# A delta-rule attention with a feed-forward layer: the planned order of the work replaced by an order laid by hand in a table

## The chip, the cores and the metric

The kernel runs on one core of a Trainium2 chip. Its time is the device time of one execution in microseconds (us). TensorE is called PE in the rows (PEld is its weight load), VectorE is DVE, ScalarE is ACT, SyncE is SP; SP issues nearly all DMAs.

## The reference

`q`, `k`, `v` are 4 sequences x 8 heads x 768 positions x 48, `beta` is 4 x 8 x 768. Each of the 32 heads keeps a 48 x 48 state; the output of every position, heads side by side, goes through a feed-forward layer.

```python
k_n = k / (norm(k) + 1e-6)
for t in range(S):
    y[t] = q[t] @ state
    state = state + beta[t] * outer(k_n[t], v[t] - state.T @ k_n[t])
x = y.transpose(0, 2, 1, 3).reshape(3072, 384)
h = x @ w_in                                    # 384 -> 2048
return maximum(0.01 * h, h) @ w_out             # 2048 -> 384
```

## The kernel before, in words

**Blocks.** The 768 positions are cut into 12 blocks of 64 (C). Within a block the recurrence is solved in closed form, which needs the inverse T of a unit-triangular 64 x 64 matrix for each of the 32 heads; from block to block only the state is carried. Block n's 256 rows (4 sequences x 64) then go through the feed-forward layer. The heads are handled in two groups (g = 0, 1) of 16.

**The chain of one block** (functions and lines of the kernel before):
- `gram` (L169): loads kq, forms the products k k^T and k q^T on PE (pg, L198, 32 matmuls a group), copies the first to gs on ACT (L202), writes its triangles to DRAM (gd, L207, four small DMAs a group) and reads them back with one head per partition as L (L222). DVE masks the second product into rq (L214) and keeps a corner in gm (L218).
- `inv` (L270): `norms` (L229 to L249, small DVE operations, from L237 on), then `eliminate` (L251): 31 steps, each of up to four DVE operations (L261 and L266). The first two blocks are inverted together, their 32 heads each filling 128 partitions with two 32 x 32 halves; every later block alone, spread over 128 partitions by halves of the rows.
- `bounce` (L305): T goes to DRAM (td; for later blocks also transposed, tt, after an ACT copy at L298).
- `merge` (L322): reads T back (rt, gm), for the first two blocks transposes it on PE (pt, L337, copied by DVE at L338), and joins the two halves by two products: pz (L354, copied to zs by ACT and DVE, L356) and pu (L364, copied into rt by ACT, L370, and DVE, L368).
- `solve` (L378): pn (L382) and nt; loads k, v, q; `kt` (pk, L407; ACT copies L409; DVE scales v at L413), `step_w` (pw, L421; copies L426), `step_s` (pc, L434; L436), `step_y` (py, L444; ys, L446).
- `columns` (L469): px (L477) turns ys into columns, split into xh (ACT, L118) and xl (DVE, L119).

**The feed-forward layer** (`ffn`, L484): 16 steps f. A step is nine ph matmuls (L504) with 256 columns, then ACT's gh and ph (L508, L509), DVE's gl (L511), and, two steps later, six po matmuls (L494) with 384 columns, whose sums stay in two PSUM banks over the block. At the block's end ACT copies po to ob (L525) and SP sends it out.

**Weights.** 16 tiles of 768 KB (`load_w`) come as 64-bit floats and are taken apart into a high and a low part by seven operations each (`weights`, L127: ACT at L140, L144, L153, DVE at L142, L146, L148, L155).

**What sets the order.** The program is traced by generators that `weave` (L536) interleaves by shares: in each block of feed-forward steps some steps of the weights, of the chain of block n + 1, of the inverse of block n + 2 and of the Grams of block n + 3. The compiler then orders each engine's instructions by a schedule that it simulates (`schedule_with_timeline_sim=True`), held by edges "issue this behind that" (`behind`, table `AFTER`). PSUM: two banks for po, two for ph, four (`ps_a`) that the chain shares.

Of the kernel before, what the change touches and what calls it, by code (L numbers as in the profile page):

```python
# [50 lines left out]
def delta_moe_kernel(ctx: ExitStack, tc, kqT, kv, qT, beta, cst, w_all, out, nblk):  # L51
# [75 lines left out]
    def weights():  # L127

        for f in range(NFC):
            raw = raws.pop(f)
            mid = raw[:, 0:8 * DO].bitcast(U32).rearrange("p (n two) -> p two n", two=2)[:, 1]
            top = raw[:, 4:].rearrange("p (n four) -> p four n", four=4)[:, 0]
            n = sb.tile([P, 2 * DO], BF16, tag="ca", name=f"ca{f}", bufs=2)
            g = sb.tile([P, 2 * DO], F32, tag="cg", name=f"cg{f}", bufs=CB)
            gi, gt = g.bitcast(U32), g.bitcast(U16).rearrange("p (n two) -> p two n", two=2)[:, 1]
            at = iter(AFTER.get(f, AFTER[None]))
            with behind(next(at)):
                nc.scalar.activation(n, top.bitcast(BF16), AF.Abs)  # L140
            with behind(next(at)):
                nc.vector.tensor_scalar(n, n, A_MIN, A_MAX, ALU.max, ALU.min)  # L142
            with behind(next(at)):
                nc.scalar.activation(g.bitcast(I32), n.bitcast(U16), AF.Copy, bias=-float(TOP_MIN << 19), scale=float(1 << 19))  # L144
            with behind(next(at)):
                nc.vector.scalar_tensor_tensor(gi, mid, 13, gi, ALU.logical_shift_right, ALU.bitwise_or)  # L146
            with behind(next(at)):
                nc.vector.scalar_tensor_tensor(gt, top, 0x8000, gt, ALU.bitwise_and, ALU.bitwise_or)  # L148
            t = sb.tile([P, 2, 2 * DO], F32R, tag=f"w{f}", name=f"w{f}", bufs=1)
            for k in range(2):  # L150
                wi[k][f], wo[k][f] = t[:, k, :DO], t[:, k, DO:]
            with behind(next(at)):
                nc.scalar.copy(t[:, 0], g)  # L153
            with behind(next(at)):
                nc.vector.tensor_tensor(t[:, 1], g, t[:, 0].bitcast(F32), ALU.subtract)  # L155
# [490 lines left out]
```

## Time and profile before

| | us |
|---|---|
| median of three runs | 697.28 (696.96 to 698.68) |
| the profiled execution | 697.9 |
| its span, first to last instruction | 696.1 |
| PE busy | 620.6 (89%) |
| DVE busy | 473.6 (68%) |
| ACT busy | 328.7 (47%) |

The profile is of one execution. Busy times are sums over the whole span; the stages differ, so the rows below are taken by stage. A row such as `384.32 0.39 PE L504 ...` gives start and length in us of a run of like instructions; matmuls overlap, so their distance is read from start to start.

### The profile page before, as it was taken

Reading aid. Unit: us, or ns where it says so; the run is one execution under the profiler, and the core shown is the slowest. Engines: PE = TensorE matmul, PEld = TensorE weight load, DVE = VectorE, ACT = ScalarE, POOL = GpSimd, SP = SyncE. Lnnn points to the kernel's source line nnn. Section 1 sums busy time; section 2 is a strip of 40 time slices with the busy share of each in tenths; the row PEclk is TensorE's granted clock in tenths of the full one; section 3 lists DMA queues with packets and bytes.
Section 4 is the critical chain, followed back from the end, with each engine's and each line's share of the span. In section 5 each row is a group of like instructions: output and inputs, shape, how many; then the busy total and the mean of one; then the engine's idle time right before and its main releaser. Section 6 shows DMA issues by size and latency. Waiting matters only on the chain.

```text
span 696.1 us, 20962 instructions
## 1 busy us (share of the span) xinstructions
PE 620.6 (89%) x8424; PEld 579.2 (83%) x8424; DVE 473.6 (68%) x2050; ACT 328.7 (47%) x811; POOL 7.4 (1%) x12
## 2 busy tenths in 40 slices
PE   4102989779999999999999999999999999999996
PEld 3102878679999999999999999999999999999996
DVE  6898599797965957947857758759759759431221
ACT  2221688424555445544634634635535544544432
POOL 4000000000000000000000000000000000000000
PEclk9999989969999999999999999999999999999999
DMA  8797611374055074072172271380370440410001
GB/s 204 179 402 146 221 25 25 69 160 67 7 92 137 4 134 97 14 146 74 36 141 57 48 150 35 61 168 5 73 157 3 82 102 3 70 24 3 12 13 24
DMA packets 126274, 60.39 MB, mean 87 GB/s; under 512 B 112992, under 2 KB 116192, under 8 KB 126176
## 3 DMA queue, kind: packets, MB, share of 16 engines
q1 hardware_dynamic: 123456, 57.86, 36.7%
q10 hardware_dynamic: 2720, 1.18, 0.9%
q8 instruction: 66, 1.08, 0.6%
q14 instruction: 32, 0.26, 0.1%
HBM read 46.70 MB, written 12.32 MB: 85 GB/s over the span
## 4 chain that ended last, share of the span: by engine, by line
PE 78%; DMA 9%; DVE 8%; ACT 2%; issue 1%; SPq 1%; ACTq 0%; DVEq 0%
PE ph L504 30%; PE po L494 27%; DMA wr<-in_w_all 5%; PE pw L421 3%; PE py L444 3%; PE pk L407 3%; PE pu L364 2%; PE pg L198 2%; DVE rv L413 2%; PE pc L434 2%; PE pz L354 2%; PE px L477 2%; DMA kq<-in_kqT 2%; DMA L<-gd 1%; DVE cg L146 1%
## 5 line engine op out<-in xcount | busy, mean ns | idle before, releaser
L504 PE MATMUL ph<-xh,w 128*128 128x256 f32 x1152 | 249.8, 291 | 5.7 <-DVE gl L511 5.6
L504 PEld LDWEIGHTS ph<-xh,w 128*128 128x128 f32 x1152 | 192.5, 191 | 13.9 <-DVE gl L511 8.0
L494 PE MATMUL po<-w,gh 128*128 128x384 f32 x768 | 191.7, 345 | 3.6 <-ACT gh L508 3.6
L511 DVE TENSOR_TENSOR gl<-ph,gh 128x256 fp32r<-128x256 f32 x192 | 81.1, 424 | 134.7 <-ACT ph L509 125.6
L504 PE MATMUL ph<-xl,w 128*128 128x256 f32 x576 | 166.1, 289 | 0.6
L508 ACT ACTIVATE gh<-ph 128x256 fp32r<-128x256 f32 x192 | 73.8, 385 | 150.3 <-PE ph L504 148.6
L494 PEld LDWEIGHTS po<-w,gh 128*128 128x128 f32 x768 | 132.6, 191 | 5.8 <-ACT gh L508 5.6
L494 PE MATMUL po<-w,gl 128*128 128x384 f32 x384 | 119.4, 343 | 0.0
L266 DVE TENSOR_TENSOR T<-T,tmp 128x60 f32<-128x60 f32 (+35 forms) x661 | 112.6, 208 | 1.3
L261 DVE TENSOR_TENSOR tmp<-T,L 128x60 f32<-128x60 f32 (+35 forms) x661 | 112.7, 208 | 0.8
L504 PEld LDWEIGHTS ph<-xl,w 128*128 128x128 f32 x576 | 110.0, 191 | 3.1 <-DVE xl L119 2.2
L509 ACT ACTIVATE ph<-ph 128x256 f32<-128x256 f32 x192 | 72.9, 380 | 0.0
L494 PEld LDWEIGHTS po<-w,gl 128*128 128x128 f32 x384 | 67.9, 189 | 0.5
L214 DVE TENSOR_TENSOR rq<-pg,csb 64x256 f32<-64x256 f32 x96 | 40.6, 423 | 18.8 <-ACT gs L202 17.6
L198 PE MATMUL pg<-kq 48*64 48x128 f32 x768 | 35.8, 306 | 13.8 <-DMA kq<-in_kqT 4.9
L198 PEld LDWEIGHTS pg<-kq 48*64 48x64 f32 x768 | 28.8, 150 | 20.2 <-DMA kq<-in_kqT 5.7
L337 PE MATMUL pt<-csb,rt 32*32 32x32 f32 x128 | 6.8, 215 | 33.3 <-DMA rt<-td 33.3
L337 PEld LDWEIGHTS pt<-csb,rt 32*32 32x32 f32 x128 | 5.9, 129 | 33.7 <-DMA rt<-td 33.4
L409 ACT ACTIVATE rt<-pk 48x512 f32<-48x512 f32 x44 | 26.1, 594 | 14.8 <-PE pk L407 14.1
L202 ACT COPY gs<-pg 128x256 f32<-128x256 f32 x48 | 15.8, 376 | 33.0 <-PE pg L198 27.0
L426 ACT COPY rv<-pw 64x384 f32<-64x384 f32 x46 | 21.8, 474 | 17.3 <-PE pw L421 16.4
L413 DVE TENSOR_TENSOR rv<-rv,nt 64x384 f32<-64x384 f32 x48 | 23.7, 555 | 8.8 <-ACT nt L384 8.7
(61 smaller groups left out, 634.4 us busy)
## 6 DMA issues: line engine op xcount, KB each, us to landing
wr<-in_w_all SPq DMA_DIRECT2D x16, 768.0 KB, 10.2
kq<-in_kqT SPq DMA_DIRECT2D x44, 192.0 KB, 4.2
L<-gd SPq DMA_DIRECT2D x22, 256.0 KB, 3.9
rk<-in_kv SPq DMA_DIRECT2D x24, 192.0 KB, 3.2
rv<-in_kv SPq DMA_DIRECT2D x24, 192.0 KB, 4.2
rq<-in_qT SPq DMA_DIRECT2D x24, 192.0 KB, 4.1
out<-ob SPq DMA_DIRECT2D x48, 96.0 KB, 2.8
rt<-td SPq DMA_DIRECT2D x48, 64.0 KB, 2.7
```

Source lines behind the costliest of these rows:

```text
L198: nc.tensor.matmul(ps[b][c * 64:(c + 1) * 64, p * 128:(p + 1) * 128], kq[r, c ^ b, p, 0], kq[r, c ^ b, p].rearrange("p x t -> p (x t)"), s ...
L214: nc.vector.tensor_tensor(qa[DN, c, b * NPAIR:(b + 1) * NPAIR], pv[b][r, 1], tri[r].rearrange("p (o t) -> p o t", o=1).broadcast_to([C, NP ...
L261: nc.vector.tensor_tensor(tv, t[:, :, j:j + 1].broadcast_to([P, k, w]), L[:, j, j + 1:].rearrange("p (o w) -> p o w", o=1).broadcast_to([P ...
L266: i = nc.vector.tensor_tensor(t, t, tv, ALU.subtract)
L409: nc.scalar.mul(t[UP, c], pv[c * 64:c * 64 + D], -1.0)
L413: nc.vector.tensor_tensor(v[DN, :, us], v[DN, :, us], nt[DN, g, :, us].rearrange("p h (u o) -> p h u o", o=1).broadcast_to([C, 2, NPAIR, D ...
L426: i = nc.scalar.copy(v[DN, c], pv[c * 64:c * 64 + C])
L494: i = nc.tensor.matmul(po[t][:, :DO], a[:, ts_], w[f], start=(f == 0 and k == 0), stop=(f == NFC - 1 and k == 2))
L504: nc.tensor.matmul(ph, a[f][:, cc * P:(cc + 1) * P], x[cc][e], start=(k == 0), stop=(k == 3 * NCC - 1))
L508: nc.scalar.activation(gh, ph, AF.Prelu, alpha=0.01)
L509: i = nc.scalar.activation(ph, ph, AF.Prelu, alpha=0.01)
L511: i = nc.vector.tensor_tensor(gl, ph, gh.bitcast(F32), ALU.subtract)
```

## The change

The generators, `weave`, `AFTER` and `behind` go. The program is traced under `tc.manual_schedule()`, so that each engine runs its instructions in the order of the text, and that order comes from a table with one entry for each feed-forward step: what stands before the bar is played ahead of the step's ph, what follows it after the step's po. Letters are chain parts, for both groups unless a digit follows, `e*3` is three steps of the inverse of block n + 2, `f` of block n + 1, `w` seven conversion steps, `@` names a block.

```diff
+    both = {
+        "A": (1, load_t), "B": (2, load_kv), "C": (1, turn), "Z": (1, merge_z), "U": (1, merge_u),
+        "V": (1, values), "K": (1, step_k), "W": (1, step_w), "S": (1, step_s), "Y": (1, step_y),
+        "P": (1, halves_a), "H": (1, halves_b), "J": (1, halves_c),
+        "G": (3, gram), "O": (3, gram_out), "R": (3, gram_rest), "M": (3, gram_corner)}
+    once = {
+        "Q": (3, loads_kq), "I": (3, gram_in), "D": (2, bounce), "N": (1, turn_norms), "X": (1, columns),
+        "F": (1, lambda n: scales(where[n][0])), "d": (1, bounce), "T": (2, bounce_turned), "t": (1, bounce_turned), "i": (2, gram_in), "c": (3, load_beta)}
...
+    for n in range(nblk):
+        plan = PLAN.get(n, STEADY)
         for f in range(NFC):
...
+            before, _, after = plan.get(f, "").partition("|")
+            play(n, before)
+            first(n, f)
             if len(pend) > PD:
-                second(*pend.pop(0))
-            yield
...
+                second()
+            play(n, after)
+    while pend:
+        second()
+
+
+PROLOGUE = (
+    "Q@0 Q@1 l@0 l@1",
+    "G0@0 O0@0 G1@0 O1@0 G0@1 O0@1 G1@1 O1@1 I@0 c@0 I@1 R0@0 R1@0 w*3", "identities", "R0@1 w*2 R1@1 w*2 M@0 M@1",
+    "l@2 B@0 l@3 l@4 l@5",
+    "w*2 e@0*1 F@0 N@0 e@0*17 D@0 D@1 V@0 A@0 l@6 l@7",
+    "l@8 l@9 l@10 l@11",
+    "w*27",
+    "P@0 w*3 H@0 w*2 J@0 w*3 Z@0 w*2 U@0 w*2 W@0 A@1 w*2 Y@0 w*4 X@0 S@0 B@1 Q@2 l@12 l@13 l@14 l@15 w*2",
+)
+PLAN = {
+    0: {0: "|w", 1: "P|w", 2: "H N c@2|w", 3: "J G0@2 O0@2 R0@2|w", 4: "Z G1@2 O1@2 R1@2 I@2|w", 5: "U|w", 6: "K V|w",
+        7: "W|w", 8: "Y S B c Q|w", 9: "|w", 10: "X|w e*1", 11: "G0 O0|e*2", 12: "|e*4", 13: "G1 O1|e*4", 14: "I|e*4", 15: "|e*4"},
+    1: {0: "|f*4", 1: "|f*4", 2: "|f*4", 3: "|f*34 d", 4: "|t", 5: "A|e*1", 6: "F|R0@3", 7: "|R1@3", 8: "Q@4|e*1", 9: "C N Z|e*3", 10: "U V|e*2", 11: "K|e*3", 12: "W|e*3",
+        13: "Y S B c|e*3", 14: "X|e*3", 15: "G0@4 O0@4 R0@4|e*3"},
+    2: {0: "G1@4 O1@4 R1@4|f*4", 1: "|f*4", 2: "I@4|f*34 d", 3: "|t", 4: "A|e*1", 5: "F Q|e*1", 6: "|e*3", 7: "|e*3", 8: "|e*3", 9: "C N Z|e*2", 10: "U V|e*2", 11: "K|e*3",
+        12: "W|e*3", 13: "Y S B c|e*3", 14: "X G0 O0 R0|e*2", 15: "G1 O1 R1|e*34 D"},
...
+STEADY = {0: "|t", 1: "A", 2: "|e*1", 3: "F|e*2", 4: "|e*2", 5: "|e*3", 6: "C N Z|e*2", 7: "U V|e*2", 8: "Q|e*3", 9: "K|e*3", 10: "W|e*3", 
+          11: "|e*3", 12: "Y S B c|e*3", 13: "X G0 O0 R0|e*2", 14: "G1 O1 R1|e*2", 15: "I|e*34 D"}
...
+        with tc.manual_schedule():
+            delta_moe_kernel(tc, *args, o, nblk)
```

In the steady blocks the PE pieces of the chain are thus seven bundles, each of both groups together: N Z, U, K, W, Y S, X G0, G1. `pend` is one list for all blocks, so that the last two po groups of a block come in steps 0 and 1 of the next.

The first pair (blocks 0 and 1) is inverted by quarters: 15 steps on two diagonal 16 x 16 pieces of each 32 x 32 half at once, instead of 31 on the whole half; three parts then join them on PE, from a corner of the Gram that ACT keeps (`M`): P (64 small matmuls a group, two copies by DVE and one by ACT), H (32, one copy by each, into T) and J (the transpose pt of before).

```diff
+    def eliminate4(L, j, T):
+        w = HQ - 1 - j
...
+        for x in range(min(j + 1, 2)):
+            t = T[:, :, x:j + 1:2, :HQ]
+            k = t.shape[2]
...
+            nc.vector.tensor_tensor(
+                tv, t[:, :, :, j:j + 1].broadcast_to([P, 2, k, w]),
+                L[:, :, j:j + 1, j + 1:HQ].broadcast_to([P, 2, k, w]), ALU.mult)
...
+    def halves_a(n, g):
...
+        for l, h, u in lu:
+            for e, a, r in quad:
+                nc.tensor.matmul(pq[a:a + HC, 0, l], t[r, h, u, a:a + HC], eye[r, r.start:r.start + HQ], start=True, stop=True)
...
+                nc.tensor.matmul(pq[a:a + HQ, 1, l], w[r, l], t[r, h, u, a + HQ:a + HC], start=True, stop=True)
...
+    def halves_b(n, g):
...
+    def halves_c(n, g):
```

Other moves: weights 0 and 1 are loaded through ACT's queue and the rest through SP's; the 16 gd transfers of the first pair all go through SP (before, half of them through ACT); the fourth Gram uses the ph banks (before, the third and the fourth both used the po banks); for blocks from 2 on all copies of Z and U are ACT's; the two output copies of a block precede its four output transfers.

## Rows read from the trace of the kernel before

**Rows 1.** The timeline of PE: start, length, line and tile; the first ph of block 0, of blocks 5 and 6, and of two successive steps of the last block.

```profile
85.62 0.38 PE L504 MATMUL ph<-xh,w 128*128 128x256 f32 x1
...
361.69 0.39 PE L504 MATMUL ph<-xh,w 128*128 128x256 f32 x1
...
411.89 0.39 PE L504 MATMUL ph<-xh,w 128*128 128x256 f32 x1
...
674.41 0.28 PE L504 MATMUL ph<-xh,w 128*128 128x256 f32 x1
...
676.51 0.28 PE L504 MATMUL ph<-xh,w 128*128 128x256 f32 x1
```

**Rows 2.** Busy time by stretch: its length, then busy us (and instructions) of PE, PEld, DVE, ACT and POOL, the granted clock as a share of full speed, the DMA engines' share and GB/s. The stretches are the first chain, block 0 in two parts, block 1 and block 5.

```profile
60.00:85.60 25.60, 19.23 (x396) 17.59 (x396) 16.46 (x26) 12.05 (x21) 0.00 (x0) 1.00 0.65 183
85.60:120.00 34.40, 31.32 (x437) 28.06 (x435) 33.40 (x56) 30.24 (x57) 0.00 (x0) 0.90 0.10 25
120.00:160.50 40.50, 31.86 (x390) 28.91 (x390) 35.27 (x155) 14.51 (x38) 0.00 (x0) 0.83 0.51 109
160.50:211.10 50.60, 50.31 (x705) 46.80 (x703) 37.03 (x194) 25.83 (x65) 0.00 (x0) 1.00 0.38 67
361.70:411.90 50.20, 49.83 (x704) 46.44 (x703) 35.95 (x176) 24.92 (x65) 0.00 (x0) 1.00 0.40 81
```

**Rows 3.** The timeline of PE in block 5: the first chain piece, a wait, the pk piece between a po and two ph, and the last of the 14 pieces.

```profile
361.91 0.61 PE L477 MATMUL px<-csb,ys 128*128 128x128 f32 x4
...
366.24 0.97 PE L494 MATMUL po<-w,gh 128*128 128x384 f32 x4 [0.29 <-ACT gh L508]
...
382.13 0.34 PE L494 MATMUL po<-w,gl 128*128 128x384 f32 x1
382.40 1.99 PE L407 MATMUL pk<-rt,rk 64*48 64x64 f32 x64
384.32 0.39 PE L504 MATMUL ph<-xh,w 128*128 128x256 f32 x1
384.55 0.28 PE L504 MATMUL ph<-xl,w 128*128 128x256 f32 x1
...
411.66 0.30 PE L382 MATMUL pn<-csb,sq 64*64 64x32 f32 x2
```

**Rows 4.** Groups of ACT's instructions in block 5 (busy us, mean ns of one, idle time before and what ended it): the copies of pk.

```profile
L409 ACT ACTIVATE rt<-pk 48x512 f32<-48x512 f32 x4 | 2.4, 594 | 1.3 <-PE pk L407 1.3
```

**Rows 5.** The timeline of PE and of DVE in the start: the last Gram with its wait, and the first operation of the first norms.

```profile
17.68 2.67 PE L198 MATMUL pg<-kq 48*64 48x128 f32 x30 [4.90 <-ACT gs L202]
...
27.57 0.18 DVE L237 TENSOR_SCALAR sr<-L 128x32 uint32<-128x32 uint32 x1
```

**Rows 6.** DMA issues of the whole run: number, KB each, median us from issue to landing, for the small Gram transfers by the queue that issued them.

```profile
gd<-gs SPq DMA_DIRECT2D x88, 32.0 KB, 2.9
...
gd<-gs ACTq DMA_DIRECT2D x8, 32.0 KB, 1.9
```

**Rows 7.** The timeline of DVE in the first inverse: first step, a step of 58 elements, a step of 128 elements, last step.

```profile
32.95 0.28 DVE L261 TENSOR_TENSOR tmp<-T,L 128x31 f32<-128x31 f32 x2
...
36.38 0.34 DVE L261 TENSOR_TENSOR tmp<-T,L 128x58 f32<-128x58 f32 x2
36.63 0.34 DVE L266 TENSOR_TENSOR T<-T,tmp 128x58 f32<-128x58 f32 x2
...
46.02 0.48 DVE L261 TENSOR_TENSOR tmp<-T,L 128x128 f32<-128x128 f32 x2
46.42 0.48 DVE L266 TENSOR_TENSOR T<-T,tmp 128x128 f32<-128x128 f32 x2
...
55.73 0.28 DVE L266 TENSOR_TENSOR T<-T,tmp 128x30 f32<-128x30 f32 x2
```

**Rows 8.** Groups of DVE's instructions in block 0, 85.62 to 160.54 us (busy us, mean ns of one, idle time before).

```profile
L148 DVE SCALAR_TENSOR_TENSOR cg<-wr,cg 128x768 uint16<-128x768 uint16 x10 | 10.5, 1052 | 0.1
L155 DVE TENSOR_TENSOR w<-cg,w 128x768 fp32r<-128x768 f32 x10 | 9.5, 945 | 0.4 <-ACT w L153 0.3
L261 DVE TENSOR_TENSOR tmp<-T,L 128x60 f32<-128x60 f32 (+29 forms) x51 | 8.7, 210 | 0.1
...
L146 DVE SCALAR_TENSOR_TENSOR cg<-wr,cg 128x768 uint32<-128x768 uint32 x9 | 8.4, 948 | 0.0
L214 DVE TENSOR_TENSOR rq<-pg,csb 64x256 f32<-64x256 f32 x16 | 6.8, 423 | 0.3
...
L413 DVE TENSOR_TENSOR rv<-rv,nt 64x384 f32<-64x384 f32 x7 | 3.5, 555 | 0.0
L142 DVE TENSOR_SCALAR ca<-ca 128x768 bf16<-128x768 bf16 x8 | 2.8, 348 | 0.0
L218 DVE COPY gm<-gs 32x256 f32<-32x256 f32 x8 | 2.3, 288 | 0.1
...
L356 DVE COPY zs<-pz 32x256 f32<-32x256 f32 x2 | 0.8, 415 | 0.0
```

**Rows 9.** The chain that ended last, in the start: the first transfer of the bounce and the first transpose behind it (start, length).

```profile
60.84 2.28 DMA td<-T
...
65.09 1.91 PE pt L337 x32
```

**Rows 10.** The timeline of PE in the first chain: the py matmuls of block 0.

```profile
77.96 3.86 PE L444 MATMUL py<-rv,rq 128*64 128x48 f32 x63
```

More of the change, by code (lines that the diff above doesn't have):

```diff
@@ L33 @@
 HC = C // 2
+HQ = HC // 2
 P = 128
@@ L127, in weights @@
[L127 to L155, printed above, removed]
-            yield
@@ new lines, in conversions, with ps @@
+    def conversions():
+        for k in range(-3, NFC):
+            for f in (k + 1, k + 2, k, k + 1, k, k + 1, k + 3):
+                if 0 <= f < NFC:
+                    if f not in conv:
+                        conv[f] = convert(f)
+                    next(conv[f])
+                    yield
+    wg = conversions()
+    betas, Xs, kqs, pgs, gss, gds, Lh, gm, nm, nrm, invs, Tts, nts, zss, ys, xs = ({} for _ in range(16))
+    def ps(x, n, g):
+        return ps_a.tile([P, 512], F32, tag="a", name=f"{x}{n}_{g}")
@@ L245, in norms @@
         nc.vector.tensor_tensor(c, c, r, ALU.mult)
-        mark[f"norms{n}"] = nc.vector.tensor_tensor(c, c, r, ALU.mult).ins
-        for e in range(2):
-            nc.scalar.mul(z[:, e * HC:(e + 1) * HC], s, half[:, e:e + 1])
+        nc.vector.tensor_tensor(c, c, r, ALU.mult)
         return c
@@ L303, in inv @@
             yield
+        for n in NB[b]:
+            Tts[n] = X, M
     def bounce(n):
         b, i = where[n]
[L308 to L320 removed]
@@ new lines, in merge_u, with scales, turn_norms @@
+            if n < 2 and h:
+                nc.vector.tensor_scalar(d, uv[h * 64:h * 64 + HC], -1.0, None, ALU.mult)
+            else:
+                nc.scalar.mul(d, uv[h * 64:h * 64 + HC], -1.0)
+    def scales(b):
+        z = sb.tile([P, C], F32, tag="sq", name=f"sq{b}", bufs=2)
+        for e in range(2):
+            nc.scalar.mul(z[:, e * HC:(e + 1) * HC], nrm[b], half[:, e:e + 1])
+        nrm[b] = z
+    def turn_norms(n):
+        b, i = where[n]
+        p = ps("pn", n, 0)
+        nc.tensor.matmul(p[DN, 0:HS], nrm[b][i * 64:i * 64 + 64], eye0[i * 64:i * 64 + 64], start=True, stop=True)
+        nts[n] = nt = sb.tile([P, NGR, 2, GU], F32, tag="nt", name=f"nt{n}", bufs=2)
+        nc.scalar.copy(nt[DN].rearrange("p g h u -> p (g h u)"), p[DN, 0:HS])
@@ L532, in chain @@
-    def chain(fn, blocks):
-        for n in blocks:
-            yield from fn(n)
-    def weave(n_slots, *streams):
-        taken = [0] * len(streams)
-        for i in range(n_slots):
-            for k, (gen, steps, a, b) in enumerate(streams):
-                want = steps if i >= b - 1 else max(0, i + 1 - a) * steps // (b - a)
-                while taken[k] < want:
-                    next(gen, None)
-                    taken[k] += 1
-    NS, NF, NI = NSLOT, NFC + 1, HC + 1
-    wg = weights()
@@ new lines, in inv_steps @@
+    def inv_steps(b, k):
+        if b < len(NB):
+            if b not in invs:
+                invs[b] = inverse(b)
+            for _ in range(k):
+                next(invs[b], None)
+    both = {
[3 more added lines that the diff above has]
+        "G": (3, gram), "O": (3, gram_out), "R": (3, gram_rest), "M": (3, gram_corner)}
```

619 lines of the change are left out of this document (305 added, 314 removed), and 3 rows, old and new, of the table PLAN.

## The prediction

> **What bounds the kernel now.** I read the profile by blocks, since twelve blocks of the same feed-forward work follow a long start. The edges are the first ph matmul of a block [rows 1]: block 0 begins at 85.6 us, and block 5 runs from 361.69 to 411.89, 50.2 us. In the last block, which carries no chain, two successive steps begin 2.10 us apart, so 16 bare steps cost 33.6 us. Next I read the busy time by stage [rows 2]. From 85.6 to 160.5 us (block 0, 74.9 us instead of 50) DVE is busy 33.4 + 35.3 = 68.7 us and TensorE 31.3 + 31.9 = 63.2: DVE sets the pace there. From block 1 on TensorE does (50.3 of 50.6 us; 49.8 of 50.2), with DVE at 36 and ACT at 25. So there are two accounts: the start and block 0, where DVE and latencies count, and the steady blocks, where only TensorE's own time counts.
>
> **Steady blocks.** Chain work in a block costs 50.2 - 33.6 = 16.6 us. None of its matmuls is removed; only the seams can go. A seam is read at the pk piece [rows 3]: its first matmul starts 0.27 us after a po that otherwise takes 0.17, and the ph after it takes 0.23 to the next instead of 0.12, so 0.2 us for going in and out. Block 5 holds 14 such pieces (px in four, pu in three, of which one is mixed with pz, pn alone, pg in two; the first and the last of the 14 are in rows 3). The table makes seven bundles of them. Of the seven seams saved, three are px pieces, at 0.14 each, and four cost 0.2: 1.2 us. The rest is TensorE's idle time, 50.2 - 49.8 = 0.4 us, chiefly the wait of 0.29 for gh at 366.24; I credit 0.3. That is 1.5 us a block, 48.7 us. Bounds: 0 (every bundle brings a new wait of the size of the old one) to 1.85 (nothing idles and every seam counts in full).
>
> What hides the rest: between two dependent bundles lies a step, ph plus po, of 2.1 us. The longest evacuation is K's, four copies of 0.59 us on ACT [rows 4]; the first starts half-way through K's 1.9 us, so the last ends 1.0 + 2.4 = 3.4 us after K begins, and W begins after 1.9 + 2.1 + seam = 4.2. The margin is 0.8 us. Moving the zs and rt copies of the second half from DVE to ACT (for n of 2 or more) adds four ACT copies, about 1.5 us to ACT's 25, which stays cover. On SP the output transfers and the T loads stand behind one another as before; the L load (I) now stands ahead of D and waits there for the gd transfers, but the reader of D's result, C, comes six steps (12.6 us) later.
>
> **Start, up to the first ph.** (1) The Grams. The last one began 4.9 us late, waiting for a PSUM buffer that ACT's gs copy released [rows 5]; the change gives the fourth Gram the ph banks, so norms could begin at 27.57 - 4.9 = 22.7 us at best, and at 27.57 if the transfers hold it. All 16 small gd transfers now go through SP, where before ACT issued 8; the median from issue to landing was 2.9 us on SP, 1.9 on ACT [rows 6]. I take 25, the middle. The trace does not show how these transfers fare when weights 0 and 1 go through ACT's queue instead of SP's. The Trainium skill, "DMA: Bandwidth & Descriptors", section "Queues, rings and completion order", says that each DMA engine alternates between the queues by packet; by that the gd pieces would no longer stand behind the weights, and norms would begin near 22.7, which takes 2.3 us off the sum; only the two medians bear on it here, and they lean its way. (2) From norms to the first elimination took 5.4 us with one conversion of 0.95 inside: 4.5. (3) Elimination. Two instructions of 58 elements start 0.25 us before the next two, two of 128 elements 0.40 [rows 7]: 0.063 us each plus 1.07 ns per element. The 31 steps had 122 instructions and 10,900 elements (19.4 us; the trace has 32.95 to 56.0 with two interruptions); 15 quarter steps have 58 and 2,720: 6.6 us, and I take 7 for the four-dimensional access. That is done at 25 + 4.5 + 7 = 36.5. (4) V, four of 0.52: 38.6. (5) The table then puts 27 conversion steps ahead of P, 16 of them on DVE, four times (0.35 + 0.95 + 0.95 + 1.05) = 13.2 us [rows 8]: 51.8. The bounce (4.3 from the first td to the first pt) and P's matmuls hide behind them [rows 9]. (6) P's DVE copies, four of 0.42, 1.7, H's matmuls and copies 2.3, and then the old chain from the first pt (65.09) to the first ph (85.62), 20.5 us, and 1.2 for conversions standing in DVE's and ACT's order before a copy: 77.5 us, **8.1 us earlier**. Bounds: 72 (norms at 22.7, nothing in line, H hidden) and 83 (norms at 27.6, the in-line conversions each late).
>
> One thing here is a choice. The clock column says 1.00 for 60 to 85.6 us, but the py matmuls of the first pair took 61 ns each where the steady pk takes 30 [rows 3, 10]; I price the chain by the durations. The Trainium skill, "TensorE: Matmul & The Clock Gate", section "Seeing it yourself", warns that recorded clock events can be wrong and says to cross-check. If the column were right instead, the added P and H would cost half, about 1.5 us less.
>
> **Block 0.** DVE: conversions before were 31.2 us; 32 of the 64 DVE conversion instructions are now placed ahead of the first ph and 32 remain (27 us): -4.2. Elimination of pair 1: 25 steps to 17, at 0.5: -4. Gram evacuations for four groups (9.1) to two: -4.5. V seven to four: -1.5. P and H copies: +2.5. So 68.7 - 11.7 = 57 us [rows 8]. TensorE: 33.6 + chain 15.1 + two more Gram groups at 1.2 + P, H and J's 256 small matmuls (0.02 to 0.04 each, 6) = 57 as well. Neither can be under 57, and two in-order engines that feed each other lose some; before, the busier one idled 6.2 us. I take 64, **10.9 us less**; bounds 58 and 71. The granted clock was 0.90 and 0.83 there, that is 6.9 + 13.8 us at 1.2 GHz; TensorE had been idle about a fifth of that time. If it is denser now, part comes back; this is in the bounds.
>
> **Sum** against the profiled run (697.9; span 696.1): -8.1, -10.9; block 1 (one Gram group fewer, and a slow start gone) 50.55 to 48.2, -2.4; block 2 (one group more) -0.3; blocks 3 to 8 -1.5 each, -9; block 9 -1.5, block 10 -1.4; the last block 0; the end +0.5, since both output copies now precede the four transfers. Together -33.1: 664.8, and as the profiled run is 0.6 above the median, **664 us**.
>
> **Rivals.** (A) The forecast, 0.62. (B) The steady seams give nothing: each block stays 50.2 and the front alone pays, 664 + 14 = 678; for it, TensorE idles only 0.4 us a block; against, seams are counted busy and fewer of them remain. 0.16. (C) The start is denser: norms at 22.7 and a block 0 of 58, 1.85 a block: 664 - 5 - 6 - 3 = 650. 0.14. (D) Slower: the 2.1 us step between dependent bundles is too short. Its place is ACT's order: if the copies of Z, U, K, W and Y end later than the next bundle's turn, TensorE stops in all five places, in ten blocks. It decides from 33/50 = 0.66 us a place beyond the present margin; at 1.3 us late it costs 65 us, 729. Against it stands K's margin of 0.8 us, where ACT's load is greatest. 0.04. (E) The hand order does not change what the engines run (the same waits set the same times) or the front's gain goes to in-line conversions: 690 to 697. 0.04.
>
> **Numbers.** 664 is A's. The range takes in B's centre and C's: 649 to 681, which leaves out D, E and the tails. A change of 0.3% (2 us) is about what a measurement of this kernel can tell. Faster by more: A, B, C and most of E, 0.94; within: 0.02; slower: 0.04.
>
> **What would show it.** First ph near 77; block 0 near 64, with DVE busy 55 to 60 of it; blocks 3 to 8 at 48.7, with seven chain pieces each and no TensorE wait above 0.3 us; the 15 quarter steps in 7 us. Waits of ph, po or a bundle on ACT copies in every block would say D; an unchanged 50.2 says B; a first ph past 83 says that the conversions ahead of P are the bound of the start.

## The result, and the profile after the change

The changed kernel takes 680.42 us, median of 4 runs (678.2 to 681.84), against 697.24 (696.96 to 698.68) for the kernel before in the same session: 0.9752 of the time, 95% interval 0.9721 to 0.9783. It is 16.8 us faster where the forecast said 33. The profiled execution took 679.8 us, its span 678.0, so it stands 18.1 us below the profiled one of before. All medians are of the fast runs; two far slower ones, a run of e8 at 1183 us and one of the kernel before in its session, are left out.

The timeline of PE after the change: the first ph of blocks 0 to 5 and 11, and of a second bare step of block 5 (start, length, line, tile).

```profile
76.16 0.38 PE L528 MATMUL ph<-xh,w 128*128 128x256 f32 x1
...
152.14 0.28 PE L528 MATMUL ph<-xh,w 128*128 128x256 f32 x1
...
201.58 0.39 PE L528 MATMUL ph<-xh,w 128*128 128x256 f32 x1
...
252.75 0.28 PE L528 MATMUL ph<-xh,w 128*128 128x256 f32 x1
...
304.04 0.28 PE L528 MATMUL ph<-xh,w 128*128 128x256 f32 x1
...
352.51 0.28 PE L528 MATMUL ph<-xh,w 128*128 128x256 f32 x1
...
354.63 0.28 PE L528 MATMUL ph<-xh,w 128*128 128x256 f32 x1
...
636.94 0.28 PE L528 MATMUL ph<-xh,w 128*128 128x256 f32 x1
```

Set against the same edges of before [rows 1], the distances give the whole account:

| stretch | before | after | change | forecast |
|---|---|---|---|---|
| start, up to the first ph | 85.62 | 76.16 | -9.5 | -8.1 |
| block 0 | 74.92 | 75.98 | **+1.1** | **-10.9** |
| block 1 | 50.55 | 49.44 | -1.1 | -2.4 |
| block 2 | 50.20 | 51.18 | +1.0 | -0.3 |
| block 3 | 50.20 | 51.29 | +1.1 | -1.5 |
| blocks 4 to 8, together | 250.98 | 242.37 | -8.6 | -7.5 |
| blocks 9 and 10 | 93.24 | 90.54 | -2.7 | -2.9 |
| block 11 and the end | 40.4 | 41.1 | +0.7 | +0.5 |
| sum | 696.1 | 678.0 | -18.1 | -33.1 |

Of the 15 us that are missing, 12.0 are missing in block 0, 3.9 in blocks 2 and 3 and 1.3 in block 1; the start and blocks 4 to 8 came 2.5 better than forecast. Block 0 is the question.

Busy time by stretch after (columns as in [rows 2]): the chain ahead of block 0, block 0 in two parts, block 1, block 5.

```profile
59.50:76.20 16.70, 15.86 (x415) 15.11 (x407) 12.33 (x21) 9.54 (x19) 0.00 (x0) 1.00 0.12 20
76.20:110.00 33.80, 27.03 (x711) 24.75 (x710) 24.80 (x45) 19.33 (x40) 0.00 (x0) 0.75 0.59 162
110.00:152.10 42.10, 38.32 (x496) 36.09 (x495) 32.04 (x100) 24.39 (x55) 0.00 (x0) 0.92 0.34 75
152.10:201.60 49.50, 48.99 (x705) 46.27 (x703) 38.73 (x199) 25.92 (x67) 0.00 (x0) 1.00 0.36 73
352.50:401.00 48.50, 48.50 (x705) 46.23 (x704) 33.97 (x174) 26.48 (x69) 0.00 (x0) 1.00 0.44 84
```

In block 0 DVE is busy 24.8 + 32.0 = 56.8 us, which is the forecast's 57. TensorE is busy 27.0 + 38.3 = 65.3, not 57, and idle for 10.6; it now sets the pace. The granted clock is 0.75 and 0.92, so it stood at the lower of its two levels for half of 33.8 and 0.16 of 42.1 us: some 24 of the 76 us ran at 1.2 GHz, more than the 20.7 that [rows 2] give for before. The view of waits says where the 10.6 us are (total, times, longest):

```profile
PE pv L390 <- issue: 4.0, 1, 4.0
PE pq L380 <- issue: 2.8, 1, 2.8
PE pk L474 <- DVE rt L436: 2.2, 1, 2.2
PE pg L188 <- DMA kq<-in_kqT: 1.6, 2, 1.1
```

The first two, 6.8 us, lie in the new parts P (pq) and H (pv), in the middle of bursts of small matmuls, and are put down to "issue": the engine waited for nothing that the profile shows. The same two tiles stop in the start as well. The timeline of PE, for the heads of block 0 ahead of it and then, inside block 0, for those of block 1:

```profile
52.86 0.58 PE L380 MATMUL pq<-rt,nm 32*16 32x16 f32 x30 [2.77 <-issue]
...
59.06 0.59 PE L390 MATMUL pv<-ds 16*16 16x16 f32 x30 [3.62 <-issue]
...
83.23 0.99 PE L380 MATMUL pq<-rt,nm 32*16 32x16 f32 x61 [2.77 <-issue]
...
86.36 0.98 PE L390 MATMUL pv<-ds 16*16 16x16 f32 x58
91.34 1.14 PE L390 MATMUL pv<-ds 16*16 16x16 f32 x70 [4.00 <-issue]
```

Within each pair exactly 128 matmuls of the trace lie from stop to stop (the stops stand before numbers 350, 478, 1114 and 1242 of the run, counted from 0): 61 + 9 ph + 58 = 128 in the last three rows. In the runs below that keep the quarters, the stops of the start and of block 0 come before these numbers or before 606 (478 + 128), wherever the parts stand in the program. A matmul is two engine instructions, PE and PEld, so that is 256. The page's part on DMA queues has a queue that fits, packets, MB and share:

```profile
q8 instruction: 72, 1.18, 0.7%
```

Its 72 packets of 16 KB against 2 x 9192 TensorE instructions make 255 a packet. Packets of it ran at 50.62, 56.48, 80.34 and 88.79 us, 1.0 to 1.3 us long, and TensorE resumed 1.2 to 1.6 us after the end of each. So at these points TensorE had used up its instructions and the next block came late. The Trainium skill, "Runtime: NRT & Kernel Launch", section "Instruction fetch mechanics", says that an engine fetches its instructions in blocks of 16 KiB (256) through a DMA queue of its own, and that crossing a block's edge is mostly hidden; the 256 agree with the trace, and the "mostly hidden" holds for all but four of the 72 packets, but the stops at these four come to 13.2 us. What the DMA engines did meanwhile (columns as before; DMA share and GB/s last):

```profile
80.00:84.00 4.00, 1.23 (x88) 1.13 (x83) 3.42 (x5) 1.20 (x3) 0.00 (x0) 0.92 1.04 203
84.00:88.00 4.00, 3.34 (x83) 2.97 (x75) 1.35 (x5) 1.90 (x5) 0.00 (x0) 0.50 1.02 222
88.00:92.00 4.00, 0.66 (x48) 0.66 (x50) 3.07 (x4) 1.71 (x3) 0.00 (x0) 0.50 1.02 413
```

They were full (1.02 to 1.04) with the loads of kq, of k, v, q and of weights 12 to 15 that SP had issued from 75.5 to 85 us. And in the same window the granted clock goes down to 0.50, just after the stop of P (at 83.4 us).

In blocks 2 and 3 (201.6 to 304 us) one wait explains the excess:

```profile
PE ph L528 <- DVE gl L534: 2.9, 5, 1.0
```

From 304 to 594 us the same view has no row at all: no TensorE wait in the steady blocks.

### The profile page after: what moved, and what is told of

Read it like the earlier page. It is cut to its first block, busy times and chain, and to the rows that moved or that the text cites. A ratio compares the mean times of both kernels' runs of the same rounds, so it can differ in the third digit from the quotient of the medians.

```text
span 678.0 us, 22510 instructions
## 1 busy us (share of the span) xinstructions
PE 614.3 (91%) x9192; PEld 582.7 (86%) x9192; DVE 443.0 (65%) x1957; ACT 350.9 (52%) x875; POOL 6.5 (1%) x12
## 4 chain that ended last, share of the span: by engine, by line
PE 74%; DVE 11%; DMA 6%; issue 3%; ACT 2%; SPq 2%; ACTq 0%; DVEq 0%
PE ph L528 28%; PE po L545 24%; PE pk L474 3%; PE py L502 3%; PE pw L482 3%; PE pg L188 2%; PE pc L492 2%; PE px L513 2%; PE pu L432 2%; PE pz L422 2%; DMA kq<-in_kqT 2%; DVE tmp L266 2%; DVE T L271 1%; DMA wr<-in_w_all 1%; DMA L<-gd 1%
## 5 line engine op out<-in xcount | busy, mean ns | idle before, releaser
L545 PE MATMUL po<-w,gh 128*128 128x384 f32 x768 | 198.4, 340 | 0.3 <-ACT ob L551 0.3
L545 PE MATMUL po<-w,gl 128*128 128x384 f32 x384 | 130.0, 339 | 0.0
L271 DVE TENSOR_TENSOR T<-T,tmp 128x60 f32<-128x60 f32 (+4 forms) x600 | 98.3, 204 | 0.7
L266 DVE TENSOR_TENSOR tmp<-T,L 128x60 f32<-128x60 f32 (+4 forms) x600 | 97.6, 203 | 0.4
L545 PEld LDWEIGHTS po<-w,gl 128*128 128x128 f32 x384 | 72.8, 190 | 0.0
L188 PE MATMUL pg<-kq 48*64 48x128 f32 x736 | 28.8, 295 | 7.4 <-DMA kq<-in_kqT 7.3
L188 PEld LDWEIGHTS pg<-kq 48*64 48x64 f32 x736 | 22.5, 144 | 12.2 <-DMA kq<-in_kqT 6.6
L482 PEld LDWEIGHTS pw<-rv,rt 128*64 128x64 f32 x768 | 24.6, 143 | 2.8 <-ACT gh L532 2.5
L474 PEld LDWEIGHTS pk<-rt,rk 64*48 64x48 f32 x704 | 22.0, 126 | 5.1 <-ACT ph L533 2.8
L502 PEld LDWEIGHTS py<-rv,rq 128*64 128x64 f32 x768 | 23.7, 138 | 2.9 <-ACT ph L533 2.5
```

The costliest lines, as they stand in the source:

```text
L188: nc.tensor.matmul(pt[b][c * 64:(c + 1) * 64, p * 128:(p + 1) * 128], kq[r, c ^ b, p, 0], kq[r, c ^ b, p].rearrange("p x t -> p (x t)"), s ...
L266: nc.vector.tensor_tensor(tv, t[:, :, j:j + 1].broadcast_to([P, k, w]), L[:, j, j + 1:].rearrange("p (o w) -> p o w", o=1).broadcast_to([P ...
L271: nc.vector.tensor_tensor(t, t, tv, ALU.subtract)
L474: nc.tensor.matmul(pv[r, u], k[DN, c, u], t[DN, c, u], start=True, stop=True)
L482: nc.tensor.matmul(pv[r, u], t[:, c, u], v[:, c, u], start=True, stop=True)
L502: nc.tensor.matmul(pv[s * C:(s + 1) * C, u * D:(u + 1) * D], qa[:, c, u], v[:, c, u], start=True, stop=True)
```

## The experiments

The theory: block 0 lost its gain because P and H stop TensorE where a block of instructions ends while the DMA queues are full ("traffic"), and because TensorE then ran half of the time at the low clock. Rivals: the small matmuls use up instructions faster than they can be fetched, whatever the queues do ("rate"); or DVE's conversions, which stand ahead of the copies that P, H and K wait for, pace the block as before.

**e1_spread: P and H of block 0 one group a step.** Each burst is half as long.

```diff
-    0: {0: "|w", 1: "P|w", 2: "H N c@2|w", 3: "J G0@2 O0@2 R0@2|w", 4: "Z G1@2 O1@2 R1@2 I@2|w", ...
+    0: {0: "P0|w", 1: "P1|w", 2: "H0 N c@2|w", 3: "H1 G0@2 O0@2 R0@2 J|w", 4: "G1@2 O1@2 R1@2 I@2 Z|w", ...
```

Expected: 

> Edit: in block 0 the parts P and H of block 1's chain are played one group per feed-forward step (P0, P1, H0, H1 in steps 0 to 3) instead of both groups at once in steps 1 and 2; J and Z stay in steps 3 and 4. Theory 'fetch': TensorE stood still for 2.8 and 4.0 us inside P and H of block 0 because it ran through 128 tiny matmuls (256 instructions with their weight loads) faster than its next 16 KB of instructions arrived. With a step of 15 long matmuls between the groups the stalls shrink to under 1.5 us each and the low clock behind them is shorter: steps 0 to 3 fall from 30.0 to 23 to 25 us, the time from 680 to 671 to 676. Rival 'copies': the stalls are waits for DVE's and ACT's in-line copies that the trace does not name; they would come with the same parts wherever these stand: 678 to 682.

Measured: 677.01 us, 0.9731 of before (0.9711 to 0.9750), between the two ranges expected. Block 0 took 68.59, though the first ph came later (78.29); in the four profiles that leave block 0 as the change made it (after, e3, e4, e6) it took 73.9 to 77.9. The stops shrank, but did not go:

```profile
81.66 0.94 PE L380 MATMUL pq<-rt,nm 32*16 32x16 f32 x61 [0.87 <-issue]
...
88.13 0.29 PE L390 MATMUL pv<-ds 16*16 16x16 f32 x6 [3.19 <-issue]
```

H's stop is still 3.2 us, now with 6 matmuls left of its group: it stands before number 1242 again, where a block of 256 instructions ends, not at a place in the program. Spreading alone isn't the cure. e1 also plays J and Z behind the Grams; what that gives was not taken apart.

**e2_whole: the first pair inverted whole, as before the change.** 31 steps, no P, H and M; all else as after.

```diff
-    "w*2 e@0*1 F@0 N@0 e@0*17 D@0 D@1 V@0 A@0 l@6 l@7",
+    "w*2 e@0*1 F@0 N@0 e@0*34 D@0 D@1 V@0 A@0 l@6 l@7",
...
-    "P@0 w*3 H@0 w*2 J@0 w*3 Z@0 ...
+    "w*5 J@0 w*3 Z@0 ...
-    0: {0: "|w", 1: "P|w", 2: "H N c@2|w", ...
+    0: {0: "|w", 1: "|w", 2: "N c@2|w", ...
```

Expected: 

> Edit: the first pair is inverted whole again (31 steps on the full halves), P, H and M are gone; everything else as in the changed kernel. Theory 'fetch': the inverse takes 12 to 13 us more, of which the start gets back P, H and the stall in H (7 to 8), so the first ph comes at 80 to 82 instead of 76.2; in block 0 both stalls go and steps 0 to 3 take 17 to 20 us instead of 30.0: in all 670 to 675. Rival 'quarters pay': P and H cost only their own matmuls, about 4 us in block 0, so the later start is not made good: 679 to 683.

Measured: 674.11 us, 0.9681 (0.9658 to 0.9705), against 0.9752 of the change with its quarters: by the ratios 5 us less, by the medians 6.3. The first ph comes at 81.84 (5.7 later), but block 0 takes 66.55 and its first four steps 18.3 us instead of 30.0. The waits of block 0, and its first 31 us:

```profile
PE pg L188 <- DMA kq<-in_kqT: 4.0, 4, 1.3
PE pk L468 <- DVE rt L430: 2.8, 1, 2.8
```

```profile
82.00:113.00 31.00, 25.61 (x401) 22.93 (x402) 29.64 (x52) 23.53 (x46) 0.00 (x0) 0.81 0.70 193
```

No stop on issue is left. DVE is busy 29.6 of 31 us: with P and H out of the way, the rival "DVE paces" becomes the next limit (K waits 2.8 us for DVE's copy of U), together with kq, which arrives late behind the weights.

**e3_burst: the same small matmuls where nothing is loaded.** In the last block 512 matmul rows of the trace are added at one step and 64 at each of eight more; their results are read by nothing.

```diff
+    def extra(f, count):
+        bx = ps("bx", f, 0).rearrange("p (x l t) -> p x l t", x=2, l=GH)
+        for i in range(count):
+            e, a, r = quad[i % 2]
+            nc.tensor.matmul(bx[a:a + HC, 0, i // 2 % GH], eye[r, r.start:r.start + HC], eye[r, r.start:r.start + HQ], start=True, stop=True)
...
+            if n == nblk - 1 and (f == 4 or f > 7):
+                extra(f, 256 if f == 4 else 32)
```

Expected: 

> Added work only, in the last block, where the chain is done and the DMA queues are nearly idle: 256 matmuls of the form of P's first loop (512 in the trace, as each is done in two) in one burst after step 4, and 32 (64 in the trace) after each of the steps 8 to 15; nothing reads them. Theory 'fetch': the burst costs 8.2 us at 16 ns each, but it stops at every 128th matmul, 3 or 4 times, for 1.5 to 3 us, so 13 to 19 us; the eight small pieces cost 1.0 to 1.3 us each and have no stop. Rival 'copies' (nothing here waits for a copy): 8 to 9 us, no stop. A third, 'traffic' (instructions come late only behind other transfers): also no stop, as nothing else is being moved.

Measured: 704.78 us (one run). The burst took 13 us. Its timeline, and two stretches of the busy time:

```profile
647.29 4.21 PE L597 MATMUL bx<-csb 32*32 32x16 f32 x232
651.93 7.07 PE L597 MATMUL bx<-csb 32*32 32x16 f32 x256 [0.43 <-issue]
659.42 0.83 PE L597 MATMUL bx<-csb 32*32 32x16 f32 x24 [0.42 <-issue]
```

```profile
647.00:651.00 4.00, 4.00 (x223) 3.75 (x223) 0.42 (x1) 0.02 (x1) 0.00 (x0) 0.94 0.01 4
...
654.00:661.00 7.00, 6.58 (x214) 6.44 (x211) 0.00 (x0) 0.00 (x0) 0.00 (x0) 0.50 0.02 5
```

With the DMA engines at 0.01 to 0.02 the stops are 0.43 and 0.42, a tenth of H's 4.0. That speaks for traffic, though it does not rule out rate: the stops are 256 rows apart, not the 128 that were expected, so every second block of instructions was there in time. The eight small pieces added 1.2 to 1.3 us each and had no stop, as expected. A second thing showed: the granted clock fell to 0.50 inside the burst, where TensorE ran nothing but these small matmuls and was busy all but 0.85 us, and a matmul went from 16 to 27 ns.

**e4_split: the price of a seam.** Z and W of the steady blocks in one piece for each group, nine pieces instead of seven.

```diff
-STEADY = {..., 6: "C N Z|e*2", 7: "U V|e*2", 8: "Q|e*3", 9: "K|e*3", 10: "W|e*3", 11: "|e*3", ...
+STEADY = {..., 6: "C N Z0|e*2", 7: "Z1|e*2", 8: "U V Q|e*3", 9: "K|e*3", 10: "W0|e*3", 11: "W1|e*3", ...
```

Expected: 

> Edit: in the steady table Z and W are played one group per step (Z0, Z1 and W0, W1 in two steps each), so that a block has nine pieces instead of seven. Theory 'seams': each more piece costs 0.2 us, blocks 4 to 8 go from 48.47 to 48.8 to 48.9 us. Rival 'idle': the steady gain of the change came from TensorE's waits, not from the number of pieces: 48.47 to 48.55.

Measured: 685.29 us (one run); blocks 4 to 8 take 49.12 each instead of 48.47, as the first ph of blocks 5 and 6 shows:

```profile
354.13 0.28 PE L528 MATMUL ph<-xh,w 128*128 128x256 f32 x1
...
403.25 0.28 PE L528 MATMUL ph<-xh,w 128*128 128x256 f32 x1
```

TensorE waits for nothing in these blocks, so two more pieces cost 0.65, 0.32 each, more than the 0.2 expected. That a piece costs TensorE time without any wait is shown, and with it the mechanism of the steady gain. The seven pieces that the change saved were cheaper: of the 1.73 us a block (50.20 to 48.47), 0.37 was idle time, which leaves 1.36, or 0.19 each. Why Z and W cost more when split stays open.

**e5_loads: kq of block 2 and weights 12 to 15 issued ahead of the chain.**

```diff
-    "l@8 l@9 l@10 l@11",
+    "l@8 l@9 l@10 l@11 Q@2 l@12 l@13 l@14 l@15",
...
-    "... A@1 w*2 Y@0 w*4 X@0 S@0 B@1 Q@2 l@12 l@13 l@14 l@15 w*2",
+    "... A@1 w*2 Y@0 w*4 X@0 S@0 B@1 w*2",
```

Expected: 

> Edit: the loads of weights 12 to 15 and of kq for block 2 stand in SP's order right behind weight 11 (issued from 44 us on, when the queues are free) instead of behind the first ph (79 to 85 us). Nothing else. In the changed kernel the DMA engines were fully busy from 80 to 92 us, exactly where TensorE stood still in P and H of block 0, and the burst of the last block with idle queues hardly stopped. Theory 'traffic': instructions come late because they queue behind these loads; with them gone the stops of 2.8 and 4.0 us fall under 1 us each, the low clock behind them is shorter, steps 0 to 3 go from 30 to 22 to 25 us and the time to 671 to 676; H of block 0's own chain (55 to 59 us) keeps its stop of 3.6. Rival 'rate': 256 instructions in a row need their 5.5 us whatever else moves: 678 to 682.

Measured: 677.28 us, 0.9716 (0.9697 to 0.9736), between the two ranges expected; first ph 79.68, block 0 69.86, its steps 0 to 3 23.7. The timeline of PE, and the stretches of two stops:

```profile
67.06 1.01 PE L422 MATMUL pz<-rt,gm 32*32 32x32 f32 x30 [2.98 <-issue]
...
86.64 1.01 PE L380 MATMUL pq<-rt,nm 32*16 32x16 f32 x61 [2.66 <-issue]
...
89.80 1.89 PE L390 MATMUL pv<-ds 16*16 16x16 f32 x128
```

```profile
64.00:68.00 4.00, 1.02 (x42) 0.95 (x38) 1.34 (x3) 0.36 (x1) 0.00 (x0) 0.50 1.02 413
...
88.00:92.00 4.00, 4.00 (x140) 3.67 (x139) 1.31 (x4) 2.46 (x5) 0.00 (x0) 0.50 0.02 4
```

One stop went with its loads. H of block 0 now ran its 128 matmuls without one, at a DMA share of 0.02 and at the same low clock as after the change (0.50). Z in the start, 64 matmuls that ran through after the change, stops for 3.0 us now that the weights move there (1.02, 413 GB/s). So the first ph comes 3.5 us later. P keeps its stop, against the expectation: k, v and q of block 1 are issued at 79 to 82 us.

**e6_due: the inverse steps of blocks 1 and 2 placed in time.** Steps left over at the end of a block (`e*34`) stood in DVE's order ahead of gl; they move into the steps of K, W, Y.

```diff
-    1: {..., 9: "C N Z|e*3", 10: "U V|e*2", 11: "K|e*3", 12: "W|e*3", 13: "Y S B c|e*3", ...
+    1: {..., 9: "C N Z|e*4", 10: "U V|e*3", 11: "K|e*6", 12: "W|e*6", 13: "Y S B c|e*7", ...
-    2: {..., 9: "C N Z|e*2", 10: "U V|e*2", 11: "K|e*3", 12: "W|e*3", 13: "Y S B c|e*3", 14: "X G0 O0 R0|e*3", ...
+    2: {..., 9: "C N Z|e*3", 10: "U V|e*3", 11: "K|e*5", 12: "W|e*5", 13: "Y S B c|e*5", 14: "X G0 O0 R0|e*2", ...
```

Expected: 

> Edit: in blocks 1 and 2 the steps of the next inverse are moved from the block's end, and from the start of the block after, into the feed-forward steps that hold the long bundles K, W and Y S (five to seven each instead of three); the number of steps is the same. Theory 'late inverse': blocks 2 and 3 took 51.2 and 51.3 us instead of 49.7 and 48.5 because DVE still had old inverse steps ahead of its gl at their start, and ph waited 0.3 to 1 us in five steps; block 2 goes to 49.7 to 50.2, block 3 to 48.5 to 49.0, the others stay. Rival: the waits come from DVE's load as such, and move with the steps: blocks 1 to 3 keep their sum of 151.9.

Measured: 677.61 us (one run). Blocks 1 to 3 take 48.89, 50.40 and 48.50, 147.8 together instead of 151.9: 4.1 us, and block 3 is then a steady block. In e1 to e5, e9 and e11, which leave these steps where they were, the three blocks took 151.6 to 153.0. That settles block 3; block 2 stays 0.5 above the forecast's 49.9, with one wait of 1.2 us for DVE's gl left. (Step 14 of block 2 has `e*3` in the changed kernel, as here; the table shown with the change has `e*2` there.)

**e7_quart and e8_whole: both repairs together, once with quarters and once whole.** e7 joins e1, e5 and e6; e8 joins e2, e5 and e6. In both, block 1's copies of Z and U go to ACT (`n < 2` becomes `n < 1`).

Expected of e7: 

> The quarters kept, with four edits together: P and H of block 0 one group per step (as in e1), the loads early (as in e5), the inverse steps of blocks 1 and 2 moved (as in e6), and the second half's copies of Z and U of block 1 on ACT instead of DVE, so that K does not wait for DVE's copy behind seven conversion steps (2.2 us). If the effects add (-4 to -7, -5, -4, -2): 661 to 667. If the front stays bound by DVE's conversions whatever TensorE waits for: 668 to 672.

Expected of e8: 

> The first pair inverted whole (as in e2), with the loads early, the inverse steps of blocks 1 and 2 moved and block 1's copies of Z and U on ACT. Block 0 of e2 was bound by DVE (busy without a gap from 82 to 113 us), so it gains from the copies (1.7 us and the wait of K, 2.8) and from the moved inverse, little from the loads: 664 to 669. If quarters without their stops are better than the whole inverse, e7 is faster than this by 2 us or more; if not, they cost what they save.

Measured: e7 673.50 us, 0.9668 (0.9647 to 0.9689), above both ranges expected; e8 666.11 (three runs), 0.9555 (0.9536 to 0.9575), as expected. The first ph of blocks 0 and 1, in e7 and then in e8:

```profile
80.46 0.39 PE L528 MATMUL ph<-xh,w 128*128 128x256 f32 x1
...
148.42 0.28 PE L528 MATMUL ph<-xh,w 128*128 128x256 f32 x1
```

```profile
80.42 0.39 PE L522 MATMUL ph<-xh,w 128*128 128x256 f32 x1
...
141.80 0.28 PE L522 MATMUL ph<-xh,w 128*128 128x256 f32 x1
```

Block 0 begins at the same time in both: what the quarter elimination saves on DVE, its P and H and two stops of 3.6 (H) and 3.3 us (Z) have used up by then. In block 0, 67.96 against 61.38, e7 pays for the P and H of block 1's heads, and for 20.5 us at the low clock against 6.8. Of those 20.5 the view by stretch shows, in e7:

```profile
84.00:104.20 20.20, 19.98 (x342) 18.31 (x346) 15.98 (x28) 11.03 (x23) 0.00 (x0) 0.50 0.07 12
```

TensorE is busy 19.98 of 20.20 us and stays at 0.50: no stop lies in this stretch to explain the low clock, and what does stays open. Side by side in one session, the quarters cost 7.4 us.

**e9_quiet and e11_quiet: P and H with idle queues.** To tell traffic from rate at P, the loads of k, v, q of block 1 (`B@1`) had to leave P's window. Both build on e5.

```diff
-    "... Y@0 w*4 X@0 S@0 B@1 w*2",
+    "... Y@0 w*4 X@0 S@0 w*2",
...
-    0: {..., 3: "J G0@2 O0@2 R0@2|w", ...
+    0: {..., 3: "B@1 J G0@2 O0@2 R0@2|w", ...
```

Expected of e9: 

> Edit: as e5, and the k, v, q loads of block 1 (1.2 MB, which filled the DMA engines from 76 to 84 us) stand in step 3 of block 0, so that P and H of block 0 run with idle queues. Theory 'traffic': neither P nor H stops for more than 0.7 us, and they run through at 12 to 16 ns a matmul until the clock falls; the stops of H and Z in the start (4 and 3 us, with the weights moving) stay. Rival 'rate': P keeps a stop of 2.5 to 3 us, as in e5, since two blocks of 256 instructions follow each other there in 4 us.

Measured: 679.05 us (one run), and inconclusive for P: SP has nothing to wait for ahead of `B@1` but free buffers, so it still issued the loads at 78.5 to 82 us. P ran at a DMA share of 0.98 (80 to 83 us) and stopped for 2.81 (0.67 over 83 to 86); H ran through at 0.02.

e11 puts `B@1` further back:

```diff
-    0: {..., 3: "B@1 J G0@2 O0@2 R0@2|w", ...
+    0: {..., 3: "J G0@2 O0@2 B@1 R0@2|w", ...
```

Expected of e11: 

> As e5_loads, but the loads of block 1's k, v and q now stand in SP's order behind the Gram transfers of block 2 (O0@2), which wait for a copy that comes at about 97 to 100 us. So P and H of block 0 both run with idle DMA queues. Theory 'traffic' (a stop is the refill of the instruction block, long only where the DMA engines are full): no stop above 0.7 us in P (pq) nor in H (pv) of block 0, steps 0 to 2 about 2.5 us shorter than in e5_loads. Rival 'rate' (the small matmuls use up their instructions faster than they are fetched, whatever the queues): P keeps a stop of 2.5 to 3 us. The time itself may gain or lose some us with the later loads (676 to 682).

Measured: 680.22 us (one run). Behind `O0@2`, which waits for a Gram's copy, the loads were issued from 103 us on. P and H of block 0, and two stretches:

```profile
85.67 0.20 PE L380 MATMUL pq<-rt,nm 32*16 32x16 f32 x3
87.33 0.99 PE L380 MATMUL pq<-rt,nm 32*16 32x16 f32 x61 [1.47 <-issue]
...
90.47 1.89 PE L390 MATMUL pv<-ds 16*16 16x16 f32 x128
```

```profile
84.00:86.00 2.00, 1.86 (x133) 1.76 (x124) 1.25 (x3) 1.88 (x3) 0.00 (x0) 1.00 0.04 8
86.00:88.00 2.00, 0.67 (x50) 0.67 (x52) 2.00 (x4) 0.00 (x0) 0.00 (x0) 0.88 0.00 0
```

P stops for 1.47 us with the queues idle. Neither number that was expected came (at most 0.7; 2.5 to 3): both theories hold a part. The 128 matmuls up to the stop took about 2 us (83.9 to 85.87); a packet of instructions ran from 84.58 to 85.86, and TensorE resumed 1.47 us after it. So some half of P's stop (1.47 of 2.77) is rate, and the rest goes with the traffic; H, which followed at the low clock, had none.

The packets give both parts a size. From the first matmul of one block of instructions to the first of the next, where a stop lies between them, it took 3.44 us in e11 and 2.97 and 4.02 in e3, with idle queues; TensorE had used up the block in 1.97, 2.54 and 3.60 us. After the change, with the loads moving, the same distance was 4.8 to 8.1 us. What grows is the time until the next packet begins: 0.6 to 1.1 us from the block's first matmul in e11 and e3, 1.9 to 5.6 after the change; the packet's own 0.9 to 1.5 us and the 1.2 to 1.6 behind it hardly differ. So a block that was used up faster than the next one came, in some 3 to 4 us, brought a stop with idle queues too (rate), and the loads added to it, 1.3 us at P (4.75 against 3.44) and more elsewhere (traffic).

The kernel is no faster: Z's stop in the start is still there, and K waits 2.8 us for DVE's copy of U.

**e10_best: what the runs pointed to.** e8, with J's copy for pair 1 and block 2's gm copies on ACT, and kq of block 3 ahead of k, v, q.

```diff
-            nc.vector.tensor_copy(m[R0 + HC:P, c]...
+            (nc.scalar.copy if n == 2 else nc.vector.tensor_copy)(m[R0 + HC:P, c]...
-        nc.vector.tensor_copy(gt_of(n, g)[0:HC], tv)
+        (nc.scalar.copy if n else nc.vector.tensor_copy)(gt_of(n, g)[0:HC], tv)
-        7: "W|w", 8: "Y S B c Q|w", ...
+        7: "W|w", 8: "Y S Q B c|w", ...
```

Expected: 

> e8 with two more things taken from DVE in block 0 and given to ACT (the copy of J, 1.3 us, for which Z waited 2.6, and the four gm copies of block 2's Grams, 1.2 us) and with kq of block 3 loaded ahead of k, v, q (G waited 1.4 us for it). Block 0 from 61.4 to 57 to 60, the time 662 to 665. If block 0 is by now bound by TensorE and its low clock rather than by DVE: 666 to 667.

Measured: 662.75 us (660.92 to 663.47), 0.9507 of before (0.9491 to 0.9523), 17.7 us below the median of the change as made, in another session. Block 0 and block 1:

```profile
80.30:138.50 58.20, 53.65 (x822) 49.69 (x820) 50.09 (x129) 46.25 (x100) 0.00 (x0) 0.97 0.44 96
138.50:187.30 48.80, 48.42 (x704) 45.95 (x702) 42.95 (x242) 25.80 (x67) 0.00 (x0) 1.00 0.39 73
```

Block 0 takes 58.2 us with TensorE idle for 4.5 and only 3.4 us at 1.2 GHz (0.97): the order by hand can give what the forecast asked of block 0, without the quarters.

## Why the forecast was right in direction and half in size

**The start: right, by errors that cancel in part.** Norms began at 25.61 (forecast 25), the first quarter step at 30.72, and V at 38.24 (forecast 36.5), as DVE's timeline shows beside [rows 5, 7]:

```profile
25.61 0.19 DVE L244 TENSOR_SCALAR sr<-L 128x32 uint32<-128x32 uint32 x1 [1.82 <-DMA L<-gd]
...
30.72 0.19 DVE L287 TENSOR_TENSOR tmq<-T,L 128x30 f32<-128x30 f32 x1
...
37.91 0.29 DVE L292 TENSOR_TENSOR T<-T,tmq 128x16 f32<-128x16 f32 x2
38.24 1.03 DVE L466 TENSOR_TENSOR rv<-rv,nt 64x384 f32<-64x384 f32 x2
```

The conversions ended at 52.0 (forecast 51.8). Then P and H took 7.5 us up to the first pt at 59.54, not 4.0, chiefly because of H's stop of 3.6 (P's, of 2.8, lay mostly under the conversions); and the chain from there took 16.6 instead of 20.5 and 1.2. Part of that is py: 63 matmuls in 2.46 us, which took 3.86 before [rows 10]; the rest was not taken apart. The Gram transfers of the first pair did land sooner (median 1.7 us for all 16; before 2.5 for the eight of SP and 1.9 for the eight of ACT), but DVE still waited 1.82 us for L. By the alternation between queues that the Trainium skill states ("DMA: Bandwidth & Descriptors", section "Queues, rings and completion order") the forecast had 22.7; norms came 2.9 us later, and no run separates the queues' part from that of the fourth Gram's new banks.

The choice to price the chain by the durations and not by the clock column was right: in e5 the column does show 0.50 from 60 to 68 us, with pt at 53 ns each, and after the change pt in block 0, where the column shows full speed, takes 32.

**Block 0: the failed step.** "P, H and J's 256 small matmuls (0.02 to 0.04 each, 6)" and "33.6" for ph and po made TensorE's 57. DVE's 57 was right (56.8). Three things were missing from TensorE's side:
- The size of the small matmuls. P and H are 384 rows of the trace in block 0 and J 64, not 256 in all; the three take 8.2 us from start to start without the stops, not 6.
- The clock. I priced ph, po at full speed, though [rows 2] showed 20.7 us of the block at 1.2 GHz, and put "if it is denser now, part comes back" into the bounds. Nothing came back (TensorE had been idle 16% of block 0 before, not a fifth, and was idle 14% of it now): some 24 us stood at 1.2 GHz, and ph and po took 39.1 us, start to start. These 5.5 are most of the surplus of 8.3 us in busy time.
- The stops on instructions, 6.8 us, for which nothing in the profile of before had a row, since no such burst ran there. I allowed 7 us of idling in all; it was 10.6.

So of the 12 us, 8.3 are busy time and 3.6 idle. Take the quarters out and the stops go with them (e2); with the loads early, the inverse in time and block 1's copies on ACT the low clock falls to 6.8 us (e8), and e10, with its three further moves, reaches the forecast's lower bound of 58. The cost that I counted as DVE steps saved came back as TensorE stops: a part of the change that I took for a gain of several us was a loss of 5 to 7 us.

**Blocks 2 and 3: a cost counted at nothing.** The steps of the inverse that hide under DVE's slack were taken to be due in time; the table leaves a batch of them to a block's end (`e*34`), ahead of gl in DVE's order. e6 gives back 3.6 of the 3.9 us, 0.8 in block 2 and 2.8 in block 3.

**Steady blocks: right.** 48.47 against 48.7, TensorE busy without a gap. The seams saved came out as read (0.19 each), though a piece added in e4 costs 0.32; a bare step takes what it took before (some 2.1 us in the last block of both kernels). Rival D is refuted: no bundle waits for a copy. Rival B's time (678) came nearest to the measured one, but its mechanism is wrong: the steady blocks paid in full, and of the front block 0 did not. That 680.42 lies inside the range at all is luck: the range reaches up to 681 to take in rival B, and the loss in block 0 that fills it was in no rival.

## What to carry to other kernels

Price an engine by its instructions, not by its busy time alone: a burst of tiny matmuls can run out of fetched instructions where a block of 256 of them ends, and the stop gets longer where loads fill the DMA engines, so either keep bulk loads away from such bursts or do the work in fewer, larger operations. A step that shortens one engine's work by adding small work to another has to be priced at that other engine's clock as the rows show it in that stage. In a table laid by hand, look at what is left for the end of a stage: it stands ahead of the next stage's work on the same engine.

## What the runs showed of the hardware that was not expected

- TensorE stopped for up to 4.0 us where a block of 256 of its instructions ended and the DMA engines were full, for 1.47 with idle queues (e11), for 0.43 in a long burst (e3). In e11 it used the block up in 1.97 us, in e3 in 2.54, and the next was there 3.44 and 2.97 us after the start.
- The granted clock fell to 0.50 in e3, and stayed there for 20 us in e7, with TensorE busy nearly all the time. No run shows what set it.
- SP runs ahead of a hand-made order: a load stands where its own waits put it, not at the step where the table names it (e9: `B@1` stood in the fourth step of block 0 and was issued from 78.5 us on, ahead of the first ph at 79.07).
